# Issuing the second row tile from ScalarE, first weights in pieces of three features, and a parameter tile of 128 rows, in an S5 + SwiGLU kernel

## The chip, the cores and the metric

One core of a Trainium2 chip runs the whole kernel. The metric is device time in microseconds. Engines are TensorE (PE; its weight loads are listed apart as PEld), VectorE (DVE), ScalarE (ACT), GpSimd (POOL) and SyncE (SP); SP and ACT also issue DMAs from queues of their own, listed as SPq and ACTq.

## The reference

```python
xn = _layernorm(x)                     # x: (1, 2048, 512), over the last axis, no weights
# A: a diagonal complex state space, 512 states
Lam_bar = exp(exp(log_dt) * Lam);  B_bar = ((Lam_bar - 1) / Lam)[:, None] * Bmat
h[t] = Lam_bar * h[t-1] + B_bar @ xn[t]
A = 2 * real(h @ Cmat.T) + xn * Dskip
# B: gated feed-forward, 512 -> 1792 -> 512
B = (silu(xn @ w1) * (xn @ w3)) @ w2
out = x + A + B
```

Inputs and output are bf16.

## The kernel before

The 2048 rows are split into four blocks of 512 rows, a block into four tiles of 128 rows; `x_blk[b]` holds a block, tile `c` being `x_blk[c // 4][:, c % 4, :]`. The 1792 hidden features are 14 groups of 128 ("feature f" below). Every block passes through layer norm, a transpose to `xnT` (width 512 in 4 pieces of 128 on the partitions), the gated products (`glu_up`: four matmuls with `w1_sb` into `g_ps`, four with `w3_sb` into `u_ps`, SiLU and copy on ScalarE, product on VectorE), the input matmuls of the state space (`ssm_in`), the scans on VectorE (`ssm_tasks`), and the output matmuls (`y_out`).

The program order is written by hand: each engine executes its instructions in the order of the calls, and semaphores carry the dependences. VectorE work of the later phases sits in a queue that `drain` empties between matmul groups at given rates.

Only the start differs from this steady pattern. Rows of block 0 are loaded by three SyncE DMAs (tile 0, tile 1, tiles 2 and 3 together, line 77). The weights come in pieces of two features and later of four (`load_w13`, lines 87 and 88), the first piece of w1 issued by ScalarE. Three parameter vectors of 512 numbers are loaded as rows of the small tile `prm` (line 101, twelve rows of 128), to be turned by one TensorE transpose (line 532) into columns, from which `par_cols` computes on ScalarE and GpSimd. `keep_warm` (line 143) issues matmuls on constants while TensorE has nothing else to do. Per tile of block 0:

- `stats` and `aggr` (lines 157 and 160, VectorE) give mean and variance, `rstd_act` (lines 164 and 165, ScalarE) the reciprocal root, `normed` (line 185, VectorE) the normalised tile;
- `turn` (line 244, TensorE) transposes it into a PSUM tile (`xt_a` or `xt_b`), and `put` (line 249, ScalarE, or 251, VectorE) copies that to `xnT`.

VectorE's order is stats and aggr of tile 0, then of tile 1, then `normed(0)` in two halves, `normed(1)`, and the statistics of tiles 2 and 3. `ahead` issues the w1 and w3 matmuls (line 364) of features 0, 1 and 2 for the tiles that are there already; their six PSUM tiles are `begun`. Eight PSUM banks are in use at that time: these six, `xt_a` and `xt_b`. `glu_up(0)` then adds tile 3 to those three features and goes on with feature 3 over all 512 rows at once.

Of the kernel before, what the change touches and what calls it, by code (L numbers as in the profile page):

```python
# [12 lines left out]
ACT = mybir.ActivationFunctionType  # L13

FP32 = DT.float32
BF16 = DT.bfloat16
P = 128
# [3 lines left out]
def kernel(  # L21
# [24 lines left out]
    nc = tc.nc  # L46
# [6 lines left out]
    CPB = TBLK // P  # L53
    NSB = TBLK // SB
    NDT = D // P
    NPT = PS // P
# [4 lines left out]
    xv = A_x[0].rearrange("(b c p) d -> p b c d", p=P, c=CPB)  # L61
    ov = out[0].rearrange("(c p) d -> p c d", p=P)

    const = ctx.enter_context(tc.tile_pool(name="const", bufs=1))
# [8 lines left out]

    x_blk = [xpool.tile([P, CPB, D], BF16, name="x_blk") for _ in range(NBLK)]

    for c0, c1 in ((0, 1), (1, 2), (2, CPB)):
        nc.sync.dma_start(out=x_blk[0][:, c0:c1, :], in_=xv[:, 0, c0:c1, :])
    nc.scalar.preload_act_table_set("natural_log_exp_and_others")
    w1_sb = const.tile([P, NDT, F], BF16, name="w1_sb")
    w3_sb = const.tile([P, NDT, F], BF16, name="w3_sb")  # L80
# [4 lines left out]
    def load_w13(f0, f1, engs=(nc.sync, nc.sync)):  # L85
        fs = slice(f0 * P, f1 * P)
        engs[0].dma_start(out=w1_sb[:, :, fs], in_=w1v[:, :, fs])
        engs[1].dma_start(out=w3_sb[:, :, fs], in_=w3v[:, :, fs])
# [6 lines left out]
        for t in range(NDT):  # L95
            nc.sync.dma_start_transpose(out=dst[:, t, :], in_=src[:, t * P:(t + 1) * P])

    prm = const.tile([3 * NPT, P], BF16, name="prm")

    def load_prm(i, src, eng):  # L100
        eng.dma_start(out=prm[i * NPT:(i + 1) * NPT, :], in_=src.rearrange("(t p) -> t p", p=P))

    load_prm(0, A_Lambda_re, nc.scalar)
    load_prm(1, A_Lambda_im, nc.scalar)
    load_w13(0, 2, (nc.scalar, nc.sync))
    load_prm(2, A_log_dt, nc.sync)
    load_w13(2, 4)
    load_w13(4, 6)
    nc.sync.dma_start(out=x_blk[1], in_=xv[:, 1, :, :])
    load_w13(6, 10)  # L110
    load_w13(10, NFT)
# [16 lines left out]
    ident = const.tile([P, P], BF16, name="ident")  # L128
# [11 lines left out]
    def keep_warm(n, width=512):  # L140
        one = nc.const_aps.tensor_like(1.0, like=ident[:, 0:1])
        for _ in range(n):
            nc.tensor.matmul(out=begun[0][0][:, :width], lhsT=one.to_broadcast([P, P]), rhs=one.to_broadcast([P, width]),  # L143
                             start=True, stop=True)
# [10 lines left out]
    def stats(c):  # L155
        sums[c] = work.tile([P, 6], FP32, name="stats", bufs=4)
        nc.vector.bn_stats(out=sums[c], in_=x_blk[c // CPB][:, c % CPB, :])  # L157
# [4 lines left out]
    def rstd_act(c0, c1):  # L162
        y = rstd_all[:, c0:c1]
        nc.scalar.activation(out=y, in_=mv_all[:, c0:c1, 1], func=ACT.Ln, bias=eps)
        nc.scalar.activation(out=y, in_=y, func=ACT.Exp, scale=-0.5)  # L165
# [15 lines left out]
    def normed(c, parts=1):  # L181
        xn = work.tile([P, D], BF16, name="xn", bufs=8)
        for i in range(parts):
            ds = slice(i * D // parts, (i + 1) * D // parts)
            nc.vector.tensor_scalar(out=xn[:, ds], in0=x_blk[c // CPB][:, c % CPB, ds], scalar1=mv_all[:, c, 0:1],  # L185
                                    scalar2=rstd_all[:, c:c + 1], op0=ALU.subtract, op1=ALU.mult)
        return xn
# [48 lines left out]
    new_xnT(0)  # L236
    xt_a = psum.tile([P, 2 * NDT, P], BF16, name="xt_ps", tag="ps")
    xt_b = psum.tile([P, 2 * NDT, P], BF16, name="xt_ps", tag="ps")
    pprm = xt_a[:, NDT, :3 * NPT]
    xn0 = xns_of[0] = {}  # L240

    def turn(c, pxt, d0=0, d1=NDT):
        for dt in range(d0, d1):
            nc.tensor.transpose(out=pxt[:, dt - d0, :], in_=xn0[c][:, dt * P:(dt + 1) * P], identity=ident)  # L244

    def put(c, pxt, eng, d0=0, d1=NDT):
        dst = xnTs[0][:, d0:d1, c * P:(c + 1) * P]
        if eng is nc.scalar:
            nc.scalar.activation(out=dst, in_=pxt, func=ACT.Copy)  # L249
        else:  # L250
            nc.vector.tensor_copy(out=dst, in_=pxt)
# [6 lines left out]
    def c4(name):  # L258
        col[name] = const.tile([P, NPT], FP32, name=f"c_{name}")
        return col[name]  # L260

    def par_cols():
        prmc = const.tile([P, 3 * NPT], FP32, name="prmc")
        nc.scalar.activation(out=prmc, in_=pprm, func=ACT.Copy)
        col["lre"], col["lim"], col["ldt"] = (prmc[:, i * NPT:(i + 1) * NPT] for i in range(3))
        nc.scalar.activation(out=c4("dt"), in_=col["ldt"], func=ACT.Exp)
        nc.gpsimd.tensor_tensor(out=c4("kr"), in0=col["dt"], in1=col["lre"], op=ALU.mult)
        nc.gpsimd.tensor_tensor(out=c4("ki"), in0=col["dt"], in1=col["lim"], op=ALU.mult)
        nc.gpsimd.tensor_scalar(out=c4("turn"), in0=col["ki"], scalar1=float(1.0 / (2.0 * np.pi)), scalar2=None,
                                op0=ALU.mult)  # L270
        tt = nc.gpsimd.tensor_tensor
        tt(out=c4("den"), in0=col["lre"], in1=col["lre"], op=ALU.mult)
        tt(out=c4("d2"), in0=col["lim"], in1=col["lim"], op=ALU.mult)
        tt(out=col["den"], in0=col["den"], in1=col["d2"], op=ALU.add)
# [87 lines left out]
    def glu_mm(b, f, w_sb, ps, ts):  # L362
        for dt in range(NDT):
            nc.tensor.matmul(out=ps[:, ts], lhsT=w_sb[:, dt, f * P:(f + 1) * P], rhs=xnTs[b][:, dt, ts],  # L364
                             start=(dt == 0), stop=(dt == NDT - 1))
# [128 lines left out]
    def ahead(w_sbs, fs, c, n=1):  # L494
        for f in fs:
            for w_sb in w_sbs:
                glu_mm(0, f, w_sb, begun[f][w_sb is w3_sb], slice(c * P, (c + n) * P))
# [16 lines left out]
    keep_warm(2, P)  # L514
    turn(1, t1)
    put(1, t1, nc.scalar)
    keep_warm(4, P)
    stats(2)
    aggr(2)
    rstd_act(2, 3)  # L520
    stats(3)
    ahead((w1_sb,), (0, 1), 0)
    ahead((w1_sb,), (0, 1), 1)
    xn0[2] = normed(2)
    aggr(3)
    rstd_act(3, 4)
    ahead((w3_sb,), (0, 1), 0, 2)
    turn(2, t2)
    put(2, t2, nc.scalar)
    xn0[3] = normed(3)  # L530
    ahead((w1_sb,), (2,), 0, 2)
    nc.tensor.transpose(out=pprm, in_=prm, identity=ident[:3 * NPT, :3 * NPT])  # L532
    par_cols()
    ahead((w3_sb,), (2,), 0, 2)
    ahead((w1_sb, w3_sb), (0,), 2)
# [61 lines left out]
```

## Time and profile before

| | |
|---|---|
| median of 3 runs | 212.17 us (212.15 to 212.43) |
| the profiled execution | 212.21 us, span 210.4 us from first to last instruction |
| busy: PE, DVE, ACT | 206.4, 172.9, 94.4 us |
| granted TensorE clock, mean | 0.999 |
| first matmul with w1 | starts at 6.16 us |
| first matmuls over 512 rows (feature 3) | start at 12.30 us |

Times in the views are microseconds from the start of the span. A busy engine is not at its peak, and matmuls overlap: a block of four 128-wide matmuls shows 0.39 us, while such blocks start 0.22 us apart. Idle time of an engine that is not on the chain of waits costs nothing.

### The profile page before, as it was taken

To read this page: it belongs to the slowest core of one execution; us is meant where nothing else is said; L and a number is where in the kernel's file an instruction comes from. 1 tells how busy PE (TensorE), PEld (TensorE's weight loads), DVE (VectorE), ACT (ScalarE), POOL (GpSimd) and SP (SyncE) were. 2 spreads that over 40 slices of the span, in tenths; PEclk is the share of its full clock that TensorE was granted. 3 is DMA by queue.
4 is the path that set the end of the run, shared out by engine and by line. 5 is a ranking of instruction groups with operands and counts; after the bars stand their busy time and mean duration, and the time that the engine had idled before them with its cause. 6 is when DMAs were issued, how large, how long until landed. Compare 5 with 4: busy or idle time off the path is not lost.

```text
span 210.4 us, 2883 instructions
## 1 busy us (share of the span) xinstructions
PE 206.4 (98%) x1039; PEld 97.6 (46%) x1039; DVE 172.9 (82%) x343; ACT 94.4 (45%) x167; POOL 5.8 (3%) x27
## 2 busy tenths in 40 slices
PE   8999999999999999999999999999999999999994
PEld 3864444444444444444444444444444444444453
DVE  4599989989999999999999999999999999121111
ACT  4799867666666200066666500036666620000000
POOL 2100320000000000000000000000000000000000
PEclk9999999999999999999999999999999999999999
DMA  6999588954000000000003100100000000000110
GB/s 175 307 351 194 103 189 260 276 123 101 0 3 0 0 25 25 28 26 0 0 0 79 25 7 18 50 28 0 2 0 0 0 3 25 26 25 25 42 36 25
DMA packets 27094, 13.69 MB, mean 65 GB/s; under 512 B 15944, under 2 KB 27080, under 8 KB 27080
## 3 DMA queue, kind: packets, MB, share of 16 engines
q1 hardware_dynamic: 26536, 13.25, 25.7%
q10 hardware_dynamic: 544, 0.26, 0.4%
q8 instruction: 8, 0.13, 0.3%
q14 instruction: 6, 0.05, 0.1%
HBM read 7.74 MB, written 2.10 MB: 47 GB/s over the span
## 4 chain that ended last, share of the span: by engine, by line
PE 96%; DVE 1%; DMA 1%; ACT 0%; issue 0%
PE g_ps L364 23%; PE u_ps L364 23%; PE y_ps L480 23%; PE y_ps L485 13%; PE bu_ps L403 13%; DMA x_blk<-in_A_x_dram 1%; DVE stats L157 1%; PE xt_ps L244 1%; ACT xnT L249 0%; DVE mv_all L160 0%; DVE o L490 0%; DVE xn L185 0%; PE g_ps L143 0%; PE xt_ps L532 0%
## 5 line engine op out<-in xcount | busy, mean ns | idle before, releaser
L364 PEld LDWEIGHTS <-w_sb 128*128 128x128 bf16 x504 | 46.5, 98 | 50.1
L364 PE MATMUL g_ps<-xnT,w_sb 128*128 128x512 bf16 (+1 forms) x256 | 58.5, 352 | 0.0
L364 PE MATMUL u_ps<-xnT,w_sb 128*128 128x512 bf16 (+2 forms) x248 | 58.4, 358 | 0.0
L480 PE MATMUL y_ps<-w_sb,hgT 128*128 128x512 bf16 (+2 forms) x238 | 51.2, 366 | 0.0
L382 ACT ACTIVATE up<-u_ps 128x512 bf16<-128x512 f32 x56 | 33.7, 602 | 15.2 <-PE u_ps L364 14.9
L405 ACT ACTIVATE u<-bu_ps 128x512 bf16<-128x512 f32 x32 | 19.1, 597 | 46.3 <-PE bu_ps L403 46.3
L380 ACT ACTIVATE sl<-g_ps 128x512 bf16<-128x512 f32 x56 | 33.7, 602 | 9.9 <-PE g_ps L364 9.1
L437 DVE TENSOR_TENSOR_SCAN ab<-r_col,h,ab 128x256 bf16<-128x256 f32 x56 | 37.7, 732 | 0.2
L480 PEld LDWEIGHTS <-hgT 128*128 128x128 bf16 x238 | 22.8, 98 | 25.9
L490 DVE TENSOR_TENSOR o<-y_ps,x_blk 128x512 bf16<-128x512 f32 (+2 forms) x17 | 11.1, 654 | 24.3 <-PE y_ps L485 24.3
L485 PE MATMUL y_ps<-ct,h 128*128 128x512 bf16 (+2 forms) x136 | 30.4, 366 | 0.0
L403 PE MATMUL bu_ps<-xnT,bt 128*128 128x512 bf16 x128 | 28.1, 379 | 0.0
L389 DVE TENSOR_TENSOR hgT<-sl,up 128x512 bf16<-128x512 bf16 x56 | 23.0, 414 | 2.1 <-ACT up L382 2.1
L485 PEld LDWEIGHTS <-h 128*128 128x128 bf16 x136 | 13.0, 98 | 14.7
L403 PEld LDWEIGHTS <-bt 128*128 128x128 bf16 x128 | 12.5, 98 | 15.1
L157 DVE BATCH_NORM_STATS2 stats<-x_blk 128x6 f32<-128x512 bf16 x16 | 10.6, 676 | 2.0 <-DMA x_blk<-in_A_x_dram 2.0
L446 DVE TENSOR_TENSOR ab<-ab,tab_s 128x2048 bf16<-128x2048 bf16 x8 | 9.8, 1223 | 0.2
L442 DVE TENSOR_TENSOR ab<-ab,tab_c 128x2048 bf16<-128x2048 bf16 x8 | 9.8, 1222 | 0.1
L419 DVE TENSOR_TENSOR ab<-u,tab_x 128x2048 bf16<-128x2048 bf16 x8 | 9.8, 1221 | 0.0
L422 DVE TENSOR_TENSOR ab<-u,tab_y 128x2048 bf16<-128x2048 bf16 x8 | 9.8, 1220 | 0.0
L194 DVE TENSOR_TENSOR x_blk<-xd,x_blk 128x512 bf16<-128x512 bf16 x16 | 6.8, 426 | 0.5
L185 DVE TENSOR_SCALAR xn<-x_blk,mv_all,rstd_all 128x512 bf16<-128x512 bf16 (+1 forms) x17 | 6.1, 401 | 1.0 <-ACT rstd_all L165 0.8
(71 smaller groups left out, 80.6 us busy)
## 6 DMA issues: line engine op xcount, KB each, us to landing
w_sb<-in_B_w_dram SPq DMA_DIRECT2D x4, 512.0 KB, 8.7
out_dram<-o SPq DMA_DIRECT2D x15, 128.0 KB, 1.7
w_sb<-in_B_w_dram SPq DMA_DIRECT2D x1, 1792.0 KB
x_blk<-in_A_x_dram SPq DMA_DIRECT2D x3, 512.0 KB, 6.7
w_sb<-in_B_w_dram SPq DMA_DIRECT2D x5, 256.0 KB, 4.4
x_blk<-in_A_x_dram SPq DMA_DIRECT2D x2, 128.0 KB, 2.1
w_sb<-in_B_w_dram ACTq DMA_DIRECT2D x1, 256.0 KB, 4.1
x_blk<-in_A_x_dram SPq DMA_DIRECT2D x1, 256.0 KB, 3.2
```

Of the source, the lines that this page charges most:

```text
L157: nc.vector.bn_stats(out=sums[c], in_=x_blk[c // CPB][:, c % CPB, :])
L364: nc.tensor.matmul(out=ps[:, ts], lhsT=w_sb[:, dt, f * P:(f + 1) * P], rhs=xnTs[b][:, dt, ts], start=(dt == 0), stop=(dt == NDT - 1))
L380: nc.scalar.activation(out=sl16, in_=g_ps, func=ACT.Silu)
L382: nc.scalar.activation(out=up16, in_=u_ps, func=ACT.Copy)
L389: nc.vector.tensor_tensor(out=hg[b][:, f, :], in0=sl16, in1=up16, op=ALU.mult)
L403: nc.tensor.matmul(out=u_ps, lhsT=bt[ri][:, dt, pt * P:(pt + 1) * P], rhs=xnTs[b][:, dt, :], start=(dt == 0), stop=(dt == NDT - 1))
L405: nc.scalar.activation(out=u16[:, :, pt, ri, :], in_=u_ps.rearrange("p (s t) -> p s t", s=NSB), func=ACT.Copy)
L419: nc.vector.tensor_tensor(out=ab[0][:, :, 0:2, :], in0=u16, in1=tab_b("x"), op=ALU.mult)
L437: nc.vector.tensor_tensor_scan(out=a[:, pt, 2 * ri + 1, :], data0=r_b, data1=a[:, pt, 2 * ri, :], initial=init, op0=ALU.mult, op1=ALU.add)
L480: nc.tensor.matmul(out=y_ps[:, ds], lhsT=hg[b][:, f, cl * P:(cl + 1) * P], rhs=w2_sb[:, f, ds], start=(f == 0), stop=False)
L485: nc.tensor.matmul(out=y_ps[:, ds], lhsT=h_tiles[i][:, pt, ri, h_ts], rhs=ct[ri][:, pt, ds], start=False, stop=(pt == NPT - 1 and ri == 1))
L490: nc.vector.tensor_tensor(out=o16[:, ds], in0=y_ps[:, ds], in1=x_blk[b][:, cl, ds], op=ALU.add)
```

## The change

Rows 128 to 255 (tile 1) are issued by ScalarE, after the first parameter load and ahead of w1; SyncE issues tile 0 and then tiles 2 and 3. The first weight pieces hold three features instead of two, so that four pieces take the place of six. The second parameter load moves behind w1. `prm` gets 128 rows, of which all are cleared first on VectorE and twelve are loaded, and its transpose is of 128 x 128. Four fill matmuls ahead of the first w1 matmuls become two, and the order of the `ahead` calls changes: w1 of feature 2 goes with features 0 and 1 for tiles 0 and 1; w3 of feature 1 goes behind the transposes of tile 2.

```diff
-    for c0, c1 in ((0, 1), (1, 2), (2, CPB)):
-        nc.sync.dma_start(out=x_blk[0][:, c0:c1, :], in_=xv[:, 0, c0:c1, :])
+    def load_rows(c0, c1, eng):
+        eng.dma_start(out=x_blk[0][:, c0:c1, :], in_=xv[:, 0, c0:c1, :])
+
+    load_rows(0, 1, nc.sync)
+    load_rows(2, CPB, nc.sync)
...
-    prm = const.tile([3 * NPT, P], BF16, name="prm")
+    prm = const.tile([P, P], BF16, name="prm")
+    nc.vector.memset(prm, 0.0)
...
     load_prm(0, A_Lambda_re, nc.scalar)
+    load_rows(1, 2, nc.scalar)
+    load_w13(0, 3, (nc.scalar, nc.sync))
     load_prm(1, A_Lambda_im, nc.scalar)
-    load_w13(0, 2, (nc.scalar, nc.sync))
     load_prm(2, A_log_dt, nc.sync)
-    load_w13(2, 4)
-    load_w13(4, 6)
+    load_w13(3, 6)
...
-    pprm = xt_a[:, NDT, :3 * NPT]
+    pprm = xt_a[:, NDT]
...
-        nc.scalar.activation(out=prmc, in_=pprm, func=ACT.Copy)
+        nc.scalar.activation(out=prmc, in_=pprm[:, :3 * NPT], func=ACT.Copy)
...
-    keep_warm(4, P)
+    keep_warm(2, P)
     stats(2)
     aggr(2)
     rstd_act(2, 3)
     stats(3)
-    ahead((w1_sb,), (0, 1), 0)
-    ahead((w1_sb,), (0, 1), 1)
+    ahead((w1_sb,), (0, 1, 2), 0)
+    ahead((w1_sb,), (0, 1, 2), 1)
     xn0[2] = normed(2)
     aggr(3)
     rstd_act(3, 4)
-    ahead((w3_sb,), (0, 1), 0, 2)
+    ahead((w3_sb,), (0,), 0, 2)
     turn(2, t2)
     put(2, t2, nc.scalar)
     xn0[3] = normed(3)
-    ahead((w1_sb,), (2,), 0, 2)
-    nc.tensor.transpose(out=pprm, in_=prm, identity=ident[:3 * NPT, :3 * NPT])
+    ahead((w3_sb,), (1,), 0, 2)
+    nc.tensor.transpose(out=pprm, in_=prm, identity=ident)
     par_cols()
     ahead((w3_sb,), (2,), 0, 2)
```

## The prediction

> **What bounds the kernel now.** I read the busy shares first, then the chain that ended last, then the timelines of the first 13 us, because the diff touches nothing after that.
>
> ```profile
> PE 206.4 (98%) x1039; PEld 97.6 (46%) x1039; DVE 172.9 (82%) x343; ACT 94.4 (45%) x167; POOL 5.8 (3%) x27
> ...
> PE 96%; DVE 1%; DMA 1%; ACT 0%; issue 0%
> ```
>
> TensorE carries 96% of the chain. The chain in order of time (start, length, what) shows where it does not:
>
> ```profile
> 0.72 2.10 DMA x_blk<-in_A_x_dram
> 2.82 0.02 issue
> 2.84 0.71 DVE stats L157
> ...
> 3.75 0.59 DVE stats L157
> ...
> 4.55 0.24 DVE xn L185
> ...
> 5.71 0.38 PE xt_ps L244 x4
> 6.09 0.23 PE g_ps L143 x4
> 6.32 0.45 PE g_ps L364 x8
> ...
> 8.91 0.11 PE xt_ps L532
> 9.02 0.54 PE u_ps L364 x4
> ```
>
> From 6.32 on every step to the last matmul is TensorE; before it the chain is: rows 0 to 127 land at 2.82, statistics of rows 0 to 127 and then of rows 128 to 255 on VectorE, normalise, transpose, copy out. So the change can only move the moment at which the dense stretch begins, and what lies inside 6.2 to 9.4. Whatever it moves goes to the end one for one. The timelines of TensorE, ScalarE and its DMA queue, for the same stretch:
>
> ```profile
> 5.92 0.39 PE L143 MATMUL g_ps<-const-bfloat16-1.0 128*128 128x128 bf16 x4
> 6.16 1.22 PE L364 MATMUL g_ps<-xnT,w_sb 128*128 128x128 bf16 x16
> 8.31 0.60 PE L364 MATMUL g_ps<-xnT,w_sb 128*128 128x256 bf16 x4
> 8.95 0.61 PE L364 MATMUL u_ps<-xnT,w_sb 128*128 128x256 bf16 x4
> 9.40 0.39 PE L364 MATMUL g_ps<-xnT,w_sb 128*128 128x128 bf16 x4
> ...
> 0.74 0.56 ACTq L101 DMA_DIRECT2D prm<-in_A_Lambda_re_dram  x1
> 1.34 0.26 ACTq L101 DMA_DIRECT2D prm<-in_A_Lambda_im_dram  x1
> 1.63 0.47 ACTq L87 DMA_DIRECT2D w_sb<-in_B_w_dram  x1
> ...
> 6.12 0.60 ACT L249 ACTIVATE xnT<-xt_ps 128x512 bf16<-128x512 bf16 x1 [0.20 <-PE xt_ps L244]
> ```
>
> A matmul 128 columns wide starts every 0.056 us (four in 0.22), one of 256 every 0.108 (eight from 7.22 to 8.09). The DMA view gives, from issue to landing, 2.1 for rows 0 to 127 (issued 0.72), 2.2 for rows 128 to 255 (issued 1.17, so landed at 3.37), 3.2 for rows 256 to 511 (1.64, landed 4.85), 4.1 for the first piece of w1 (1.63, landed 5.73).
>
> **Gain: the third feature.** The first eight w1 matmuls take rows 0 to 127 and should end at 6.16 + 8 x 0.056 = 6.61, but those of rows 128 to 255 start only at 6.77 (timeline in narrow windows): they wait 0.16 us for the ScalarE copy that starts at 6.12 and lasts 0.60. Afterwards twelve start at 6.05, two fill matmuls (0.11) sooner, and end at 6.72; the copy still holds the next ones until 6.77, a wait of 0.05. So four matmuls, 0.22 us, move out of the dense stretch into fill and wait. From 6.77 the rest is 12 x 0.056 + 4 x 0.108 + 0.22 (transposes) + 0.43 + parameters + 0.43.
>
> **Gain: the parameter transpose.** Its neighbours are blocks of four: one starts at 8.31 and needs 0.43, the next starts at 8.95, so the 12-row transpose takes 0.21. A full 128 x 128 transpose in this stretch costs 0.056. Whether it is the 12-row form or its three DMA waits that cost 0.15 the trace does not say; the saving is 0 to 0.16, and I take 0.15 since the full shape lets the weight load run ahead as everywhere else. Both gains: 0.22 to 0.38, and I take 0.37.
>
> **Cost: rows 128 to 255 come later.** The 128-row tile is cleared by a VectorE memset, and the first parameter load, now the first DMA of ScalarE's queue, waits for it. Prices: 0.06 us (VectorE's 128x1 memset at 0.79) and 0.21 (GpSimd's 128x128); I take 0.1, near the first as it is the same engine. VectorE is idle until 2.84, so the memset costs it nothing; it is the queue behind the wait that pays: parameter, rows 128 to 255, w1. The parameter issue begins at 0.85 to 1.00 instead of 0.74 and takes 0.26 to 0.56 (the two rows above), so the rows are issued at 1.15 to 1.60, middle 1.4, against 1.17. Also rows 256 to 511 are now issued ahead of them on SyncE at 1.17. First bytes flow some 1.1 us after an issue (80 GB/s over 1.5 to 2.0, 234 after it), and rows land some 0.45 after their last byte at 250 GB/s, as both timed row loads fit. So rows 128 to 255 are active at 2.5 beside 256 to 511; at half the 250 GB/s the 128 KB take 1.05 us, and with the 0.45 they land at 4.0. Statistics of these rows began at 3.67 with 0.30 spare; normalising rows 0 to 127 is queued behind them on VectorE, so all of the start moves by d = 4.0 - 3.65 = 0.35. Bounds: 0 (no sharing: 1.15 + 2.2 = 3.35) and 0.75 (all 256 KB go ahead: 2.5 + 1.0 + 0.5 + 0.45 = 4.45).
>
> [...]
>
> **Cost: the first piece of w1 lands later.** ScalarE's ring now holds 128 KB of rows and 384 KB of w1, where it held 256 KB. Summing the DMA rates by half microseconds (80, 234, 252, 176, 298, 277, 339, 349, 324, 294 GB/s from 1.5 on): 157 KB by 2.5, then both rings share, 2 x 524 KB, reached at 6.15; with 0.45 the landing is W = 6.6. Two rings may fill the dip at 3.0 to 3.5, then 6.4. Bounds: 5.8 (issued at 1.7, the 4.1 of before) and 7.5 (the extra 256 KB at half of 300 GB/s on top of 5.8). TensorE wants it at 6.05 + d = 6.4. So the twelve start at the later of the two: 6.6 by W, or 6.4 by d. With the start at 6.6 the copy of rows 128 to 255, done at 6.77 + 0.35 = 7.12, is hidden behind the twelve (7.27). The later start costs 6.6 - 6.05 = 0.55; against it stand the gain of 0.37 and the wait of 0.05 at the copy, which is gone: +0.13.
>
> **What hides the rest.** Rows 256 to 511, 0.47 sooner, were 0.6 early already (4.85 against 5.47). The second parameter load is issued behind w1 and, in the built order, waits for the landing of rows 0 to 127 (2.82) on a reused semaphore; ScalarE's next work is at 3.79, so 0.41 is spare even at 0.56 of issue; without that cover each excess delays the first reciprocal root. Parameters land behind the weights, near 7, for a use at 8.5. w3's first piece, 384 KB, is issued 0.48 sooner and wanted at 7.7; the SyncE ring is then some 0.5 behind W. The later SyncE pieces are two DMAs fewer; w1 for feature 6, issued at 6.60, lands at 13.2 for a use at 17.5, so its new wait for w3's landing has 4 us of cover. The first SiLU (11.39, result 11.99) frees a PSUM bank that is wanted at 12.30: 0.3 spare, about 0.2 if TensorE gets there by 0.37 sooner.
>
> **Forecast.** The profiled execution took 212.21 us (span 210.4, 1.8 around it), against the median 212.17. 212.21 + 0.13 = 212.34. 0.2%, about what a measurement of this kernel can tell from no change, is 0.42 us: no change that shows.
>
> **Rivals.** (1) Slower by a new wait at one place: TensorE's queue stands at the first w1 weight load, with all matmuls behind it. It shows once W is past 6.05 + 0.42 + 0.42 = 6.89. For: w1 stands behind one more wait and 128 KB of rows, and is half as large again. Against: the middle sum lies 0.29 short of that. Price at W = 7.2: 1.15 - 0.42 = +0.73, 212.94. The delay d alone, at most 0.75, cannot get there. (2) The clock: early 512-wide matmuls start 0.43 apart, later ones 0.216. The idle stretch before the first transpose (4.55 to 4.84) grows by d, and W leaves another. If TensorE fell to half rate for as long as its start took, some 3.5 us, it would lose 1.75, so 214.0. Against: idle of 0.30 and 0.19 between 4.5 and 5.7 left the spacing at 0.056 in before. [...] (3) The edit does what it seems to: both loads in time, the whole 0.38 kept, 211.83; it shows as faster only if the parameter transpose or the remaining 0.05 gives a little more. For: 0.30 of cover at the statistics and 0.32 at w1 (5.73 against 6.05). Against: 256 KB more in the same ring.
>
> **Chances.** Forecast (within 0.42) 0.48; (1) 0.33; (2) 0.05; (3) 0.14, of which 0.11 faster and 0.03 same. Faster 0.11, same 0.51, slower 0.38. The range: low 211.8 is the whole gain; high 213.1 takes in (1) to W = 7.36 and leaves out its tail and (2); the forecast case alone reaches 211.85 to 212.6.
>
> **What would show it.** In the changed trace: the clearing memset ahead of ScalarE's first DMA; rows 128 to 255 issued near 1.4 and the second statistics starting near 4.0 with a DMA as releaser; the first w1 matmul near 6.6 released by a DMA; twelve matmuls of rows 0 to 127 followed without a gap; about 0.06 between the blocks around the parameter transpose; the first 512-wide block at 12.30 + 0.13. I am wrong if the second statistics still start at 3.67 and w1 is in place (then 3), or if W is past 6.89 (1), or if 128-wide matmuls after 6 us start 0.107 apart.

## The result, and the profile after

The changed kernel takes 214.97 us (median of 4 runs, 214.20 to 216.07) against 212.21 us: a ratio of 1.0131, 95% interval 1.0112 to 1.0149. It is slower by 2.8 us, outside the predicted range, and its runs spread over 1.9 us where those of before spread over 0.3. The profiled execution took 215.32 us, span 213.5.

The timelines of the changed kernel (start, length, engine and line, tiles) for ScalarE's DMA queue, VectorE and TensorE (the DMA queues of SyncE and ScalarE are called their rings below):

```profile
0.94 0.55 ACTq L105 DMA_DIRECT2D prm<-in_A_Lambda_re_dram  x1
1.52 0.43 ACTq L77 DMA_DIRECT2D x_blk<-in_A_x_dram  x1
1.99 0.45 ACTq L90 DMA_DIRECT2D w_sb<-in_B_w_dram  x1
...
2.93 0.69 DVE L161 BATCH_NORM_STATS2 stats<-x_blk 128x6 f32<-128x512 bf16 x1 [2.00 <-DMA x_blk<-in_A_x_dram]
4.44 0.69 DVE L161 BATCH_NORM_STATS2 stats<-x_blk 128x6 f32<-128x512 bf16 x1 [0.60 <-DMA x_blk<-in_A_x_dram]
...
5.64 0.54 PE L248 MATMUL xt_ps<-ident,xn 128*128 128x128 bf16 x4 [1.10 <-DVE xn L189]
8.04 2.23 PE L368 MATMUL g_ps<-xnT,w_sb 128*128 128x128 bf16 x24 [1.11 <-DMA w_sb<-in_B_w_dram]
12.13 0.22 PE L536 MATMUL xt_ps<-ident,prm 128*128 128x128 bf16 x1
12.19 0.60 PE L368 MATMUL u_ps<-xnT,w_sb 128*128 128x256 bf16 x4
15.53 1.03 PE L368 MATMUL g_ps<-xnT,w_sb 128*128 128x512 bf16 x4
```

Rows 128 to 255, issued at 1.52, land at 4.42, and VectorE's second statistics wait 0.60 for them (3.67 before). TensorE is idle for 1.10 us ahead of the first transpose and for 1.11 ahead of the first w1 matmul, which starts at 8.04 instead of 6.16. The parameter transpose takes 0.06 between its neighbours. The first 512-wide block starts at 15.53 instead of 12.30: 3.23 us later.

The chain of waits no longer runs through the rows' statistics. It goes from ScalarE's queue through the landing of w1, 6.0 us after its issue:

```profile
1.52 0.43 ACTq L77
1.96 0.03 issue
1.99 6.01 DMA w_sb<-in_B_w_dram
8.00 0.05 issue
8.04 2.23 PE g_ps L368 x24
```

The table of stretches of the changed kernel (in each: length, then busy time and instructions of PE, PEld, DVE, ACT and POOL, then the granted clock, DMA share, GB/s) has a second loss in its clock column:

```profile
8.50:8.70 0.20, 0.20 (x7) 0.20 (x5) 0.00 (x0) 0.20 (x1) 0.00 (x0) 0.83 1.10 328
8.70:8.90 0.20, 0.20 (x6) 0.20 (x4) 0.00 (x0) 0.17 (x2) 0.00 (x0) 0.50 1.09 334
11.90:12.00 0.10, 0.10 (x3) 0.03 (x2) 0.00 (x0) 0.10 (x1) 0.00 (x0) 0.50 1.14 358
12.00:12.10 0.10, 0.10 (x2) 0.10 (x1) 0.00 (x0) 0.10 (x1) 0.00 (x0) 0.77 1.14 369
```

From 8.63 to 12.05 the clock is at half (0.83 over a stretch of 0.20 us puts the fall 0.07 before its end). So the 3.23 us are made of three terms: the first w1 matmul starts 1.88 later (8.04 against 6.16); the work from there to the first 512-wide block is shorter by 0.32 (mainly the wait of 0.16 and 0.15 of the parameter transpose); and that work, 6.14 - 0.32 = 5.82 us at full rate, took 15.53 - 8.04 = 7.49, so the clock cost 1.67.

### The profile page after: what moved, and what is told of

Same layout as the page of the kernel before. It is cut to its first block, busy times and chain, and to the rows that moved or that the text cites. A ratio compares the mean times of both kernels' runs of the same rounds, so it can differ in the third digit from the quotient of the medians.

```text
span 213.5 us, 2886 instructions
## 1 busy us (share of the span) xinstructions
PE 207.8 (97%) x1041; PEld 98.7 (46%) x1041; DVE 173.0 (81%) x344; ACT 94.4 (44%) x167; POOL 5.9 (3%) x27
## 4 chain that ended last, share of the span: by engine, by line
PE 95%; DMA 3%; ACT 0%; ACTq 0%; DVE 0%; issue 0%
PE g_ps L368 23%; PE u_ps L368 23%; PE y_ps L484 23%; PE y_ps L489 13%; PE bu_ps L407 13%; DMA w_sb<-in_B_w_dram 3%; ACT L81 0%; PE xt_ps L248 0%; ACTq L77 0%; DVE o L494 0%; PE xt_ps L536 0%
## 5 line engine op out<-in xcount | busy, mean ns | idle before, releaser
L368 PEld LDWEIGHTS <-w_sb 128*128 128x128 bf16 x508 | 47.6, 100 | 51.4 <-DMA w_sb<-in_B_w_dram 1.3
L368 PE MATMUL u_ps<-xnT,w_sb 128*128 128x512 bf16 (+2 forms) x248 | 59.2, 363 | 0.0
```

## The experiments

Comparisons are with runs of the kernel before on the same chip. Its median there was 212.25 for experiments 4 to 7, which ran on a chip of their own, and 212.44 for the others but the last.

**1. Rows 128 to 255 back on SyncE.** The rest of the change stays.

```diff
     load_rows(0, 1, nc.sync)
+    load_rows(1, 2, nc.sync)
     load_rows(2, CPB, nc.sync)
...
-    load_rows(1, 2, nc.scalar)
```

> The changed kernel with one part undone: rows 128 to 255 are issued by SyncE again, between rows 0 to 127 and rows 256 to 511; w1's first piece (three features) stays on ScalarE's queue. Theory A (what stands on ScalarE's ring is starved while SyncE's ring is full, so every byte on it is late): the second statistics start at 3.67 again, the first transpose at 4.84, and w1, without 128 KB ahead of it, lands about 0.9 earlier than 8.0, near 7.1; the start is later by 1.05, so 212.2 + 1.05 - 0.42 = 212.8 us at full clock, and up to 1.7 more if the clock still falls. Theory B (both rings share evenly and only the larger volume is late): w1 lands near 6.3, 212.1 us. Theory C (the row move is the whole loss): time of the kernel before or below.

Measured: 212.58 us, ratio 1.0014 (0.9998 to 1.0031). The second statistics start at 3.79 with no wait, w1 lands at 6.51, and TensorE waits 0.24 us for it:

```profile
3.79 0.66 DVE L161 BATCH_NORM_STATS2 stats<-x_blk 128x6 f32<-128x512 bf16 x1
...
6.55 1.51 PE L368 MATMUL g_ps<-xnT,w_sb 128*128 128x128 bf16 x24 [0.24 <-DMA w_sb<-in_B_w_dram]
```

The move of the rows carries nearly the whole loss; by the interval it may carry all of it. For w1's landing the volume sum of theory B (6.3) is nearer than A's 7.1; the median lies between the times of the two. Rows 256 to 511, beside w1, landed at 6.2 instead of 4.85, and VectorE waited 0.60 us for them. That cost TensorE nothing in this profile: from the first w1 matmul to the first 512-wide block (12.40) it took 5.85 us, about the 5.82 of full rate. The profiled run is one of the faster ones (212.17 us); the slowest of the ten, 214.12 us, has a mean granted clock of 0.992, so the loss of clock can come here too.

**2. w1 and w3 exchanged between the queues.**

```diff
-    load_w13(0, 3, (nc.scalar, nc.sync))
+    load_w13(0, 3, (nc.sync, nc.scalar))
```

> The changed kernel with the first pieces of w1 and w3 exchanged between the queues: w1 on SyncE, w3 on ScalarE; rows 128 to 255 stay on ScalarE. The bytes are the same. Theory A (ScalarE's ring starves): w1 lands near 5.7 as w3 did, w3 near 8.0 as w1 did; the start is then set by the rows (landing 4.42, start near 6.8), w3 is wanted at 8.15 and just there; 212.2 + 0.77 - 0.42 = 212.6 us if the clock holds, since one idle stretch of 1.1 us is left. Theory B (volume and issue order): w1 lands no earlier than 7.5 and the time stays at 214 to 215.

Measured: 213.97 us, ratio 1.0061 (1.0043 to 1.0079). By the DMA view w1, on SyncE, lands 4.4 us after its issue at 1.64 (6.04), and w3, on ScalarE, 5.2 after 1.98 (7.18). With the same bytes, w1 is 2 us earlier than in the first profile of the change, as A says. But the exchange moves two things at once, the ring and the order: w1 is now issued ahead of w3 (1.64 against 1.98), where it came behind it (1.99 against 1.64). So it does not show that the ring counts. And the time is 1.4 above A's figure (one of the seven runs, 212.52 us, is at it): the rows still land at 4.43, and the clock was lost in another way. This is the timeline and one row of the table of stretches:

```profile
7.11 2.77 PE L368 MATMUL g_ps<-xnT,w_sb 128*128 128x128 bf16 x24
...
7.00:8.00 1.00, 1.00 (x12) 1.00 (x11) 0.76 (x2) 0.83 (x3) 0.00 (x0) 1.00 1.09 339
```

The 24 matmuls take 2.56 us until the next block at 9.67, 0.107 each: half rate, as in the first fill, while the clock column says 1.00. TensorE had not yet come to full rate by then. The column does not show that: in the first profile of the change too it reads 1.00 over the fill, whose matmuls start 0.43 apart, and the first clock record of that trace begins only at 5.22.

**3. Four more fill matmuls in the second idle stretch.**

```diff
     put(1, t1, nc.scalar)
     keep_warm(2, P)
+    keep_warm(4)
```

> The changed kernel with four more 512-wide fill matmuls on constants (0.86 us at full clock) behind the two that stand ahead of the first w1 matmul; loads unchanged. If the fall of the clock to half from 8.66 to 12.05 comes from TensorE's idle stretches (4.54 to 5.64 and 6.94 to 8.04), then with the second filled the first w1 matmul still starts at 8.04 but the clock stays full: 215.0 - 1.7 = 213.3 us. If the first stretch alone decides, or the fall has nothing to do with idle time, it stays at 215.0 us.

Measured: 213.20 us, ratio 1.0034 (1.0021 to 1.0047), four runs within 0.26 us, all at full clock. In its profile w1, loaded as in the change, landed at 6.9 and the fill itself held the start to 7.64. The 24 matmuls then took 1.34 us to the next block, so the clock was full. The first 512-wide block starts at 13.47, later by the start alone: 7.64 - 6.16 - 0.32 = 1.16; the profiled runs differ by 1.0 (213.22 against 212.21). With w1 there at 6.9 the second idle stretch would have been short without the fill too, so this profile alone does not show what filling it does.

**4. The change once more.**

> The changed kernel itself, unaltered, beside the others of this group. Its first profile had w1's first piece land at 8.0 and the clock at half from 8.66 to 12.05; with four fill matmuls added and the same loads w1 landed at 6.9 and the clock stayed full. If the landing on ScalarE's ring moves from run to run, this one shows another landing between 6.5 and 8.0, and times spread over more than 1 us. If the clock's fall is caused by the second idle stretch, it shows again wherever that stretch is near 1 us (214 to 216 us) and not where w1 lands before 7.2 (212.7 to 213.2 us).

Measured: 214.10 us (213.44 to 214.37), ratio 1.0083 (1.0069 to 1.0098). Its chain and timeline differ from the first profile:

```profile
1.52 3.60 DMA x_blk<-in_A_x_dram
...
7.80 2.27 PE L368 MATMUL g_ps<-xnT,w_sb 128*128 128x128 bf16 x24
```

Rows 128 to 255 landed at 5.12, w1 at 7.58, and the rows set the start. Of the 24 matmuls some 15 ran 0.107 apart, until about 9.4. So both loads and the clock move from run to run; that is the spread. The loss of clock here did not need the second idle stretch: with a first one of 1.80 us TensorE had not come to full rate before 9.4.

**5. Pieces of two features, with the rows still on ScalarE.**

```diff
-    load_w13(0, 3, (nc.scalar, nc.sync))
+    load_w13(0, 2, (nc.scalar, nc.sync))
...
-    load_w13(3, 6)
+    load_w13(2, 4)
+    load_w13(4, 6)
... (order of the matmuls and four fill matmuls as before)
```

> The changed kernel with one part undone: weight pieces of two features, the matmul order and four fill matmuls as before; rows 128 to 255 on ScalarE and the 128-row parameter tile stay. If the row move is a loss of its own: rows land at 4.42, everything up to the first w1 matmul is 0.77 later (6.93), the parameter transpose gives 0.15 back: 212.4 + 0.77 - 0.15 = 213.0 us at full clock, more if the longer idle stretch costs the clock. If the larger w1 piece is the loss: at the kernel before, 212.3 us.

Measured: 214.25 us, ratio 1.0081 (1.0052 to 1.0110). The rows land at 4.35; the 256 KB of w1 land 4.2 after 1.99, at 6.19, long before TensorE wants them at 7.24. From 7.24 the 16 matmuls took 1.65 us instead of 0.89. So the row move alone, with weights in time (the parameter tile, left in, costs nothing by experiment 6), costs as much as the whole change on that chip, by late rows (1.08 later at the first w1 matmul) and lost clock (0.76 there).

**6. The 128-row parameter tile alone**, on the kernel before.

```diff
-    prm = const.tile([3 * NPT, P], BF16, name="prm")
+    prm = const.tile([P, P], BF16, name="prm")
+    nc.vector.memset(prm, 0.0)
... (transpose of 128 x 128; second parameter load behind w1)
```

> The kernel before with the 128-row parameter tile alone: cleared on VectorE, first parameter load, w1, then the second parameter load on ScalarE; rows and pieces as before. The 12-row transpose took 0.21 us of TensorE; if the form is the reason the blocks around it close to 0.056 and the time falls by 0.15 to 212.3 us; if its three DMA waits are the reason it stays at 0.21 and 212.4 us. w1 is issued at 1.52 behind the cleared tile instead of 1.63, no loss.

Measured: 212.05 us, ratio 0.9994 (0.9985 to 1.0003). The blocks close up, 8.65 and 8.70 where 0.21 lay between: it is the form, not the three waits. The time is not separable from no change.

```profile
8.21 0.60 PE L365 MATMUL g_ps<-xnT,w_sb 128*128 128x256 bf16 x4
8.65 0.22 PE L533 MATMUL xt_ps<-ident,prm 128*128 128x128 bf16 x1
8.70 0.60 PE L365 MATMUL u_ps<-xnT,w_sb 128*128 128x256 bf16 x4
```

**7. Rows 128 to 255 first in ScalarE's queue.**

```diff
-    load_prm(0, A_Lambda_re, nc.scalar)
     load_rows(1, 2, nc.scalar)
     load_w13(0, 3, (nc.scalar, nc.sync))
+    load_prm(0, A_Lambda_re, nc.scalar)
```

> The changed kernel with rows 128 to 255 and then w1 as the first DMAs of ScalarE's queue and both its parameter loads behind them, so neither waits for the memset nor for a parameter load: rows issued near 0.74 instead of 1.52, w1 near 1.2 instead of 1.99. If the place in the queue is the reason for the loss: rows land near 3.2, rows 0 to 127 up to 0.3 later than 2.9, w1 lands 0.8 earlier: 212.2 to 212.7 us. If ScalarE's ring is starved whatever the order, the second statistics still wait for a DMA past 4.0: 213 us or more.

Measured: 212.14 us (211.94 to 213.54), ratio 1.0007 (0.9992 to 1.0022). Issued at 0.75, the rows land at 3.45 and the statistics do not wait; rows 0 to 127 land at 3.19, 0.37 later than before. So the place in the queue, 0.77 us of it, undoes the loss of the rows. w1 is no better for its early issue in the profile taken: issued at 1.20, it landed at 7.26. By the DMA view ScalarE's ring moved 0.36 MB, nearly all of w1, from 3.5 to 5.0, and the last 0.02 MB trailed from 5.0 to 7.0 beside 0.65 MB of SyncE's.

**8. Two more fill matmuls in the first idle stretch** of the change.

```diff
     xn0[0] = normed(0, 2)
+    keep_warm(2)
     turn(0, ta, 0, H)
```

> The changed kernel with two more 512-wide fill matmuls (0.86 us at half rate) between the first fill and the first transpose, that is in the first idle stretch (4.54 to 5.64 in the first profile); loads unchanged. In the repeat of the changed kernel the first w1 matmuls ran 0.107 apart till about 9.4, and mean times spread from 213.4 to 216.1. If this first stretch keeps TensorE from reaching its full rate, the w1 matmuls now start 0.056 apart and the time falls to that of the late loads alone, 212.7 to 213.5 us with a spread under 0.5. If only the stretch before w1 matters (filled before: 213.2 us), half rate still shows in some runs and the spread stays over 0.6.

Measured: 212.90 us, ratio 1.0030 (1.0013 to 1.0046). The profile has both loads late (4.45 and 7.81) and still full rate:

```profile
7.86 1.51 PE L368 MATMUL g_ps<-xnT,w_sb 128*128 128x128 bf16 x24 [0.84 <-DMA w_sb<-in_B_w_dram]
```

Two of its ten runs show a lower mean granted clock (214.38 us at 0.992, 217.41 at 0.984), so the clock can still be lost, and the spread is not under 0.5. With either fill the ratio is 1.003, where the unaltered change had 1.0131 and 1.0083 in other groups of runs; it was not run beside the fills, and w1 may have landed at other times in the runs that were not profiled. So the fills point to idle TensorE as what loses the clock, but how much of the 0.5% is clock is not shown.

**9. All rows and first weights on SyncE, in the order of need; only parameters on ScalarE.**

```diff
     load_rows(0, 1, nc.sync)
+    load_rows(1, 2, nc.sync)
     load_rows(2, CPB, nc.sync)
...
-    load_rows(1, 2, nc.scalar)
-    load_w13(0, 3, (nc.scalar, nc.sync))
+    load_w13(0, 3)
...
-    load_prm(2, A_log_dt, nc.sync)
+    load_prm(2, A_log_dt, nc.scalar)
```

> The changed kernel with all rows and both first weight pieces on SyncE's queue in the order of need (rows 0-127, 128-255, 256-511, w1, w3), and the three parameter loads alone on ScalarE's. Theory A (a byte is late when it stands on the other ring): rows 128 to 255 land at 3.37, w1 after 896 KB of one ring at 250 to 300 GB/s, 5.3 to 6.0, in time for 6.05; w3 near 7.0 for 7.4; the gain of the new matmul order and parameter transpose is kept: 212.2 - 0.4 = 211.8 us. Theory B (volume): w1 is late by the 128 KB at any place, 6.5 or later, and the time is 212.3 or more.

Measured: 211.98 us, ratio 0.9979 (0.9970 to 0.9989). w1 lands at 6.0 and no matmul waits for a load:

```profile
6.06 1.56 PE L368 MATMUL g_ps<-xnT,w_sb 128*128 128x128 bf16 x24
7.46 0.60 PE L368 MATMUL u_ps<-xnT,w_sb 128*128 128x256 bf16 x4
```

> The version with all rows and first weights on SyncE's ring and the parameters alone on ScalarE's, again, on the chip of the next one: 0.998 of the kernel before as in its first run, near 211.9 us.

The repeat missed: 212.29 us, ratio 1.0002 (0.9985 to 1.0020). In its profile w1 landed at 6.2 and the first w1 matmul started at 6.24, 0.18 later than in the first, and w3 landed at 8.09, for which TensorE waited 0.38.

**10. The same with two short fill matmuls ahead of the first transpose.**

```diff
     xn0[0] = normed(0, 2)
+    keep_warm(2, P)
     turn(0, ta, 0, H)
```

> The same version with two more 128-wide fill matmuls ahead of the first transpose (0.21 us of its 0.32 idle). If TensorE reaches full rate earlier, the first transposes (0.65 us for four in the version without) shrink to 0.54 and the slowest of its runs (212.8) go: 211.7 to 211.9 us. If not, no change against it.

Measured: 212.02 us, ratio 0.9983 (0.9971 to 0.9995). The transposes still took 0.65 us, so the fill did not do what it was put there for; its profile waits 0.16 for w3. In two of three measurements this order lies 0.2% below the kernel before, in the third it does not.

**11. Rows 256 to 511 issued later.**

```diff
-    load_rows(2, CPB, nc.sync)
...
     load_rows(1, 2, nc.scalar)
+    load_prm(2, A_log_dt, nc.sync)
+    load_rows(2, CPB, nc.sync)
```

> The changed kernel with one exchange in SyncE's queue: its parameter load goes ahead of rows 256 to 511, so that these are issued near 1.6 instead of 1.17, just behind rows 128 to 255 (1.52 on ScalarE). Left out here: every DMA transpose (B, C and the normalised rows of blocks 1 to 3) is a plain copy of the same bytes; the first is issued past 11 us, so only the first 9 us are read and its total time says nothing. If rows 128 to 255 are late because 256 KB issued earlier on the other ring pass first, they now land at 3.5 to 4.0 instead of 4.4 to 5.1. If ScalarE's ring is slow by itself, they still land at 4.4 or later. w1 has the same bytes ahead and lands between 6.5 and 8.0 either way.

Measured, in one profile: the rows, issued at 1.53, land at 4.15, w1 at 8.57. The rows gain 0.2 to 1.0 against the six landings of the unaltered order of rows (4.35, four near 4.43, and 5.12), which is later than the 3.5 to 4.0 of the first reading and earlier than the 4.4 of the second. The DMA view shows what passed first here: from 2.6 to 3.4 us ScalarE's ring moved 0.12 MB and SyncE's 0.06, where in the change SyncE's moved 0.19 MB from 2.0 to 3.0 and ScalarE's next to nothing. So rows 256 to 511 passed first in the change and second here, which speaks for the order of issue. One profile does not settle how much time it costs.

## Why the prediction was wrong

**What held.** The dense stretch did begin later, and what was lost there went to the end. The gains had the right size: the parameter transpose fell from 0.21 to 0.06, and the wait for the copy of rows 128 to 255 was gone (in the first profile behind the wait for w1, in the repeat behind the twelve matmuls of rows 0 to 127, as forecast). The memset cost 0.11 us, ScalarE's first DMA began at 0.94, and the covers named for w3, the later pieces and the second parameter load (2.92, done before 3.87) held.

**What failed.** Two steps: the even split of the two rings, which gave both d = 0.35 and W = 6.6, and the reading of the idle times by which rival (2), the clock, got 0.05 and a price of its own.

**The size of d.** I took 0.35 with bounds of 0 and 0.75, on the sum that two rings halve the rate. Measured: 0.77 in the first profile, 1.47 in the repeat. The issue time was 0.12 later than my middle; the rest is the sharing. The upper bound was the right case, all 256 KB ahead (its landing of 4.45 makes 0.80, not 0.75), and the first profile agrees with it: by the DMA view ScalarE's ring moved 0.02 MB from 3.0 to 3.5 us and 0.11 from 3.5 to 4.0, behind SyncE's rows, and the rows landed at 4.42. In the repeat ScalarE's ring moved only 0.01 MB from 4.0 to 4.8, the last of these rows, beside 0.27 of SyncE's. The 1.47 of the repeat is beyond the upper bound too.

**The size of W.** I took 6.6, with 5.8 and 7.5 as bounds; the landings of this load behind the rows were 8.0, 6.9, 7.6 and 7.8. The same sum had been tested in the working only on rows that had one ring nearly to themselves. That w1 of before landed 0.9 later than rows of the same size, issued in the same moment (5.73 against 4.85, issued at 1.63 and 1.64), stood in the profile, and I drew nothing from it. It was a sign that loads on two rings need not move side by side. The DMA view of the changed kernel shows what the even split had wrong. q1 holds SyncE's loads and q10 ScalarE's (packets, MB, share of the 16 engines), from 4.0 to 5.0, from 5.0 to 6.0 and from 6.5 to 7.0 us:

```profile
q1 hardware_dynamic: 454, 0.34, 103.0%
q10 hardware_dynamic: 15, 0.01, 3.1%
...
q10 hardware_dynamic: 435, 0.33, 100.3%
q1 hardware_dynamic: 35, 0.02, 6.0%
...
q1 hardware_dynamic: 212, 0.16, 99.0%
q10 hardware_dynamic: 11, 0.01, 4.4%
```

The two rings took turns by whole loads, in the order of issue: w3 (384 KB, issued at 1.64) passed first, then nearly all of w1 (issued at 1.99). The bulk of w1 was through about when the sum said, but its last packets trailed beside SyncE's next load until 7.5, and it landed at 8.0, after the last of them. In experiment 3 no packet of ScalarE's ring was left after 6.5, and the same load landed at 6.9. So the sum missed the turn and the tail; that ScalarE's ring is the weaker one is not shown, since in experiments 2 and 7 too the load that was issued first passed first, whichever ring it stood on. Rival (1), the wait at the first w1 load past 6.89, was the right mechanism, with 0.33.

**The clock.** Rival (2) had 0.05. I argued from idle of 0.30 and 0.19 us that had left the spacing at 0.056, but the case to be judged had two stretches of 1.1, and the reading was wrong for the first of the two: TensorE was still at half rate there (the fill before it 0.43 apart) and the clock record of full rate begins only at 5.22. Rivals (1) and (2) were also priced apart, though the wait of (1) is the idle time of (2). Together they are the loss: 1.88 of late start and 1.67 of clock in the profiled run, less the gain of 0.32. Experiments 3 and 8 speak for idle time as the cause of the lost clock: with the same loads and TensorE filled, both profiles run the w1 matmuls at full rate.

The size was near the price: rival (2) took some 3.5 us at half rate, from the start of before, and 1.75 for it; the half-rate stretch lasted 3.42 (8.63 to 12.05) and cost 1.67. TensorE was not idle all the while before it: in the 3.4 us ahead of the fall it was busy for some 1.8 us by the table of stretches, in two places.

**What stays open.** What sets the split between the two rings. Where first loads of the two rings were issued 0.3 us or more apart they passed in the order of issue, but for such tails; in experiment 1 w1 and rows 256 to 511, issued 0.11 apart, moved side by side (0.26 and 0.27 MB from 4.0 to 5.5). No fixed share of the two rings fits all landings, and why the last packets of a load trail in some runs and not in others is not shown. Nor is what decides when TensorE comes to full rate: behind the same first idle stretch of 1.10 to 1.11 us the first four transposes took 0.54 in the first profile and in experiment 3, but 0.65 in experiment 2, where the spacing turned only at 10.0. The higher ratio of the changed kernel's first measurement (1.0131 against 1.0083 in the second) is not explained beyond the spread of landings and clock.

## What to carry to other kernels

Two queues that issue DMAs were not two equal halves of the bandwidth here (SyncE's moved 0.34 MB and ScalarE's 0.01 from 4.0 to 5.0 us of the changed kernel, 0.02 and 0.33 from 5.0 to 6.0): the load that is needed first should be issued first, with nothing else ahead of it on either ring, and a late landing should be bounded by the worst pair of landings in the trace, not by an even split. When a change lets TensorE stand idle early on, price the wait and the clock together (1.88 and 1.67 us in the first profile), because the wait makes the idle time. With a few fill matmuls there the profiles of experiments 3 and 8 ran at full rate, 24 w1 matmuls in 1.34 and 1.35 us, but the fill has a price when the load comes early: in experiment 3 it held the start 0.7 us beyond the landing. This kernel, with its start on two racing rings, also spread from run to run: 214.20 to 216.07 us, against 212.15 to 212.43 before.

## What the runs showed of the hardware

In the first profile half rate for 3.4 us (8.63 to 12.05) followed two idle stretches of 1.1 us within 3.5 us (4.54 to 5.64 and 6.94 to 8.04). TensorE was filled until 4.54 in each of five profiles, in the first without a pause from 0.76, and yet came to full rate at different times: by its clock record at 5.22 in the first, by the spacing of the matmuls only at 8.8 (experiment 5), 9.4 (4), 10.0 (2) and later than 11.0 (in experiment 11, where 23 w1 matmuls start from 8.61 to 11.0), behind idle stretches of 0.8 to 1.8 us. The mean granted clock of those four read 1.00, and only the spacing, 0.107 against 0.056 us, told it. The clock records of the first profile change at 5.22, 8.63 and 12.05, steps of 3.41 and 3.42 us. The same load from the same queue landed at 6.9 to 8.0 us in profiles of the same order of DMAs.
